# Attention and Mish FFN on one core: two weight pieces in turn on VectorE, gl moved from GpSimd to VectorE, chunk 2's normalising and moves spread over steps

## The chip, the cores and the metric

One Trainium2 chip, one of its cores. The kernel is one launch. The metric is the device time of that launch in microseconds, the median of several runs; times of single instructions come from one profiled execution, whose clock starts at the first instruction. TensorE multiplies matrices, VectorE, ScalarE and GpSimd work on whole tiles, SyncE only issues DMAs here. Each engine works its own instructions in the order of the program, and waits on semaphores for what others make.

## The reference

Windowed attention (each position sees itself and the 63 before it), then a feed-forward layer with Mish. Eight sequences of 576 positions, eight heads of 64.

```python
scores = (1 / sqrt(D)) * q @ k.T                    # per batch and head
mask   = (rel >= 0) & (rel < 64)                    # rel = pos[:, None] - pos[None, :]
attn   = softmax(where(mask, scores, -1e9))
x      = (attn @ v).transpose(0, 2, 1, 3).reshape(4608, 512)
h      = x @ w_in                                   # 512 x 2048
g      = h * tanh(softplus(h))                      # Mish
out    = g @ w_out                                  # 2048 x 512
```

## The kernel before

**Tiles.** The 4608 tokens are twelve chunks of 384. A chunk's attention runs over four pairs of heads: scores on TensorE into PSUM (`s_ps`), mask and row maximum on VectorE (`masked`: the instruction on `s_ps` and `mask`, shown as ISA in the order of instructions and as CUSTOM_DVE in the profile), exponentials on ScalarE (`exp`), normalising on VectorE (`normal`: two small instructions on `sm` and one on `pr`), a transpose, and the products with v (`o_ps`). The result is split into a high part `xh` and a low part `xl`.

**The feed-forward layer** is made in steps, one for each chunk c and each of 16 slices f of 128 hidden units. A step's input products are twelve matmuls (`h_ps`: xh with the high weights, xl with the high ones, xh with the low ones) into one of two PSUM banks with the tag "h_ps". `function` makes of them on ScalarE `t` (Mish) and `gh` (Mish, rounded to the matmul's type), and the residue `gl = t - gh` on GpSimd. Two steps later `flush` adds the step's nine output products to `acc` (gh with the high weights, gh with the low ones, gl with the high ones).

**Weights** come as 64-bit words in 32 pieces of 128x512 (`st`, three buffers) and are made into float pieces in stages, spread over the steps:

- `w_load` issues a piece's DMA on SyncE;
- `w_abs` takes the absolute bits of the high word (`wa`, a buffer of the tag "t" with four buffers, which `t` and `o` share);
- `w_bits` has four parts on VectorE, each working in place on `wa`: 0 and 1 are TENSOR_SCALAR, 2 and 3 SCALAR_TENSOR_TENSOR, of which part 3 is the last reader of `st`;
- `w_round` is ScalarE's copy into the high weights (`wi_h`, `wo_h`);
- `w_rest` is VectorE's subtraction that gives the low weights (`wi_l`, `wo_l`).

**The order.** In the head, units u = 0 to 7 are the attention of chunks 0 and 1, and pieces are worked in between. Then 32 steps of chunks 0 and 1 alternate (numbers n = 0 to 31 below; "step n" is one turn of the last loop). While `held[0]` is set, which it is for these 32, each engine's instructions keep the order in which the code issues them. A turn runs: the step's input products, t, gh and gl; `w_round`, `w_bits`, `w_abs`, `w_load`; a flush; `between(n)`; `w_rest`. In `between`, the attention of chunk 2 is made: at steps 8, 11, 17 and 20 (SCORES) the score products of one pair are put into both h banks and a second flush follows; VectorE reads them out (`masked`); at every second of these ScalarE makes both pairs' exponentials and VectorE normalises both. At 14, 17, 22 and 24 (MOVED) VectorE transposes one pair in blocks of 32 and SyncE moves the blocks with twelve DMAs (`pT<-tr`). The values of chunk 2 follow at steps 29 to 31 and after. From step 32 on a planner puts the attention of later chunks between the steps; the change leaves that code alone.

Of the kernel before, what the change touches and what calls it, by code (L numbers as in the profile page):

```python
# [10 lines left out]
F32 = mybir.dt.float32  # L11
# [4 lines left out]
ALU = mybir.AluOpType  # L16

P = 128
BLK = 64
# [8 lines left out]
def tile_window_attn_mish_ffn(  # L28
# [11 lines left out]
    NPAIR, _, NT = qT.shape  # L40
    NF, _, NC_, _ = w_in.shape
# [44 lines left out]
    pTs = [const.tile([P, P // 32, HM, 32], F32, name=f"pT{i}") for i in range(2)]  # L86
    for t in pTs:
        nc.gpsimd.memset(t, 0.0)
    pTs = itertools.cycle(pTs)
# [4 lines left out]
    held = [True]  # L94
# [17 lines left out]
    vec, act, pool, load = (InTurn(e) for e in (nc.vector, nc.scalar, nc.gpsimd, nc.sync))  # L112
# [10 lines left out]
    def acc_bank(t, name):  # L123
        return ps_acc.tile([P, CH], F32, name=name, tag=f"acc{t}")
# [107 lines left out]
        second = probs(c, s_ps[1], late)  # L232
        return [probs(c, s_ps[0], BY_HEAD), second]

    def moves(pT, tr):
        return [load.dma_start(pT[k:k + 32, r // 32, :, :], tr[r:r + 32, k // 32, :, :])
                for r in range(0, P, 32) for k in range(0, P, 32) if 0 <= k - r % BLK <= BLK]

    def run_transpose(pr, pT=None):
        tr = mp.tile([P, P // 32, HM, 32], F32, name="tr", tag="st", bufs=3) if pT is None else             ap_.tile([P, P // 32, HM, 32], F32, name="tr", tag="v_t", bufs=2)  # L240
        pT = pT or next(pTs)
        vec.transpose(tr.rearrange("p k j i -> p j k i"), pr.rearrange("p j (k i) -> p j k i", i=32))
        return pT, moves(pT, tr)

    def spare_pT():
        pT = mp.tile([P, P // 32, HM, 32], F32, name="pT", tag="st", bufs=3)
        pool.memset(pT, 0.0)
        return pT
# [28 lines left out]
    def att_transpose(pr):  # L277
        pT = next(pTs)
        tr = ap_.tile([P, P // 32, HM, 32], F32, name="tr", tag="pr", bufs=2)
        vec.transpose(tr.rearrange("p k j i -> p j k i"), pr.rearrange("p j (k i) -> p j k i", i=32))  # L280
        return pT, moves(pT, tr)

    def te_transpose(pr, banks):
        pT = next(pTs)
# [29 lines left out]
    def function(h_ps):  # L314
        t = mp.tile([P, CH], F32, name="t", tag="t", bufs=4)
        gh = mp.tile([P, CH], F32R, name="gh", bufs=3)
        gl = mp.tile([P, CH], F32R, name="gl", bufs=3)

        with tc.high_priority(offset=SOON):
            act.activation(t, h_ps, AF.Mish)  # L320
            act.activation(gh, h_ps, AF.Mish)
            pool.tensor_tensor(gl, t, gh.bitcast(F32), ALU.subtract)
        return gh, gl

    def ffn_out(acc, gg, f):
        gh, gl = gg
# [31 lines left out]
    loaded, worked, rounded = [], [], []  # L358

    def w_load():  # L360
        if pieces:
            fn, f = pieces.pop(0)
            loaded.append(fn(f))

    def w_abs(by_act):

        if not loaded:
            return
        st, wh, wl, first = loaded.pop(0)
        words = st.bitcast(U32).rearrange("p (n two) -> p n two", two=2)  # L370
        lo, hi = words[:, :, 0], words[:, :, 1]
        a = mp.tile([P, WP], U32, name="wa", tag="t", bufs=4)
        af = a.bitcast(F32)
        if by_act:
            act.activation(af, hi.bitcast(F32), AF.Abs)
        else:
            vec.tensor_scalar(a, hi, 0x7FFFFFFF, None, ALU.bitwise_and)
        worked.append((lo, hi, a, af, wh, wl))

    def w_bits(parts=range(4)):  # L380

        if not worked:
            return
        lo, hi, a, af, wh, wl = worked[0]
        for part in parts:
            if part == 0:
                vec.tensor_scalar(af, af, BIG, TINY, ALU.min, ALU.max)
            elif part == 1:
                vec.tensor_scalar(a, a, 3, 0x3FFFFFFF, ALU.logical_shift_left, ALU.bitwise_and)
            elif part == 2:  # L390
                vec.scalar_tensor_tensor(a, hi, 0xC0000000, a, ALU.bitwise_and, ALU.bitwise_or)
            else:
                vec.scalar_tensor_tensor(a, lo, 29, a, ALU.logical_shift_right, ALU.bitwise_or)
                rounded.append([af, wh, wl, False])
                worked.pop(0)

    def w_round():
        for r in rounded:
# [4 lines left out]
    def w_rest():  # L403
        while rounded and rounded[0][3]:
            af, wh, wl, _ = rounded.pop(0)
            vec.tensor_tensor(wl, af, wh.bitcast(F32), ALU.subtract)


    class Att:
        def __init__(self, c):  # L410
# [20 lines left out]
            self.load(p + 2, "qk")  # L431

        def transpose(self, p):
            self.pT[p] = att_transpose(self.pr.pop(p))

        def values(self, p, bank=at_bank, then_load=True):
            with in_order():
# [24 lines left out]
            self.pT[p] = te_copies(*self.pT[p], by)  # L462

        def dve_transpose(self, p, spare):
            self.pT[p] = run_transpose(self.pr.pop(p)[0], spare_pT() if spare else next(pTs))

        def run_scores(self, p):
            ps = (p, p + 1)
# [4 lines left out]

        def run_transpose(self, p):
            for q in (p, p + 1):
                self.pT[q] = run_transpose(self.pr.pop(q))

        def run_values(self, p):
            ps = (p, p + 1)
# [54 lines left out]
    U = len(units)  # L534
# [15 lines left out]
    def values_of(u):  # L550
        a, p = units[u]
        o_ps = (at_bank if u == U - 1 else lambda n: acc_bank(2, n))("o_ps")
        outs[u] = o_ps
        with in_order():
            value_products(a.v[p], a.pT.pop(p), [o_ps[:, n:n + BLK] for n in range(0, CH, BLK)])
        if u + 2 < U:
            a.load(p + 2, "v")
# [38 lines left out]
    for u in range(U + 1):  # L596
        now = u < U
        if u > 1:
            rest_high(u - 2)
        if now:  # L600
            a, p = units[u]
            squares_ = BY_PAIR if u == 0 else BY_HEAD
            a.masked(p, squares_, exps=False)
            exp(a.pr[p], squares_[:4])
        if u == 0:
            w_abs(False)
        if u > 1:
            rest_low(u - 2)
        if u + 1 < U:
            products_of(u + 1)  # L610
        if u > 0:
            units[u - 1][0].te_copies(units[u - 1][1], (act.copy, act.copy))
            values_of(u - 1)
        if u >= EARLY and len(early) < HEAD:
            early.append(first_half(len(early)))
        if now:
            exp(a.pr[p], squares_[4:])
        if u == U - 1:
            for n, h_ps in enumerate(early):
                step(n, h_ps)  # L620
        w_bits([0])
        w_rest()
        w_bits([1, 2])
        n = normal_parts(u) if now else iter(())
        next(n, None)
        w_bits([3])
        next(n, None)
        if u == U:
            rest_high(u - 1)
            rest_low(u - 1)  # L630
        if u + 1 not in WITHOUT:
            w_abs(u + 1 < U)
            w_load()
        next(n, None)
        w_round()
        if now:
            a.te_transpose(p, [at_bank("t_ps") if u == U - 1 else acc_bank(h, "t_ps") if u == U - 2 else h_bank("t_ps") for h in range(2)])
# [11 lines left out]
    third = atts[2]  # L649
    SCORES = [8, 11, 17, 20]  # L650
    MOVED = [14, 17, 22, 24]

    def between(n):

        if n in SCORES:
            p = SCORES.index(n)
            third.products(p, [h_bank("s_ps") for _ in range(2)])
            third.load(p + 2, "qk")
            with in_order():
                flush()  # L660
            third.masked(p, BY_HEAD, exps=False)
            if p % 2:
                third.exp(p - 1)
                third.exp(p)
                third.normal(p - 1)
                third.normal(p)
        if n in MOVED:
            p = MOVED.index(n)
            third.dve_transpose(p, p > 1)

    for n, (c, f) in enumerate(steps):
        held[0] = n < starts[2] // 2
        if n >= starts[2] // 2 and f == 0:

            while any(fn.__self__ is atts[c] for _, _, fn, _ in events):
                run(events[0][0])
        if n == starts[2] // 2:
            held[0] = True
            third.values(NPAIR - 1, h_bank)
            with in_order():  # L680
                flush()
            held[0] = False
        if n >= HEAD:
            step(n)
        run(2 * n)
        if held[0]:
            w_round()
            w_bits()
            w_abs(False)
            w_load()  # L690
            if last - 3 <= n < last - 1:
                third.load(n - last + 3, "v")
            if last < n < last + NPAIR:
                third.values(n - last - 1, h_bank)
        if len(pend) > LAG:
            with in_order():
                flush()
        if held[0]:
            between(n)
            w_rest()  # L700
        run(2 * n + 1)
    while pend:
        with in_order():
# [36 lines left out]
```

## Time and profile before

| | us |
|---|---|
| median of 3 runs | 942.03 |
| lowest to highest | 940.72 to 942.58 |
| the profiled execution's own time | 941.38 |
| its span, first to last instruction | 939.6 |
| TensorE matmul busy | 904.7 (96%) |
| VectorE busy | 315.8 (34%) |
| ScalarE busy | 397.1 (42%) |
| GpSimd busy | 204.1 (22%) |

Busy shares are over the whole span, and matmuls overlap, so TensorE's 96% doesn't say how near its peak it is. The profile's chain of waits goes through TensorE for 85% of the span, through VectorE for 8%, through DMA and SyncE for some 4%.

### The profile page before, as it was taken

What the parts mean: (1) busy time and instruction counts of PE and PEld (TensorE: products, weight loads), DVE (VectorE), ACT (ScalarE), POOL (GpSimd) and SP (SyncE); (2) the same over time, 40 slices, a digit from 0 to 9 for tenths busy, and PEclk for the clock granted to TensorE, in tenths of its full rate; (3) what the DMA queues carried; (4) which work ended last, traced back from release to release, by engine and by line L of the source; (5) the groups of instructions that cost most, each with busy time, mean ns of one, the idle gap of its engine ahead of it and who ended that gap; (6) DMA issues with size and microseconds to landing.
All of it is one profiled execution on the core that took longest, in us unless ns stands there. A gap on an engine that the chain in (4) does not pass through costs nothing.

```text
span 939.6 us, 16749 instructions
## 1 busy us (share of the span) xinstructions
PE 904.7 (96%) x6384; PEld 810.8 (86%) x6384; DVE 315.8 (34%) x1022; ACT 397.1 (42%) x1116; POOL 204.1 (22%) x211
## 2 busy tenths in 40 slices
PE   4698989999999999999999999999999999999998
PEld 3587979888889999889989999999998999999997
DVE  6989898313330330321321312303303213210000
ACT  5852626236642542542533524525525425432211
POOL 1021213222212122212222122221222122222221
PEclk9899989999999999999999999999999999999999
DMA  7744342232231321321222213203202312200000
GB/s 252 243 137 152 109 146 96 53 111 92 85 90 52 93 75 59 88 79 60 84 69 74 80 37 108 76 22 123 78 26 89 112 26 83 81 26 1 34 1 34
DMA packets 84943, 78.44 MB, mean 83 GB/s; under 512 B 11136, under 2 KB 76160, under 8 KB 84864
## 3 DMA queue, kind: packets, MB, share of 16 engines
q1 hardware_dynamic: 79680, 67.94, 23.7%
q10 hardware_dynamic: 5184, 9.44, 2.7%
q8 instruction: 51, 0.84, 0.4%
q14 instruction: 28, 0.23, 0.1%
HBM read 56.10 MB, written 9.44 MB: 70 GB/s over the span
## 4 chain that ended last, share of the span: by engine, by line
PE 85%; DVE 8%; DMA 2%; ACT 2%; SPq 2%; issue 1%; ACTq 0%
PE h_ps L115 40%; PE acc L115 38%; DVE wa L106 6%; PE o_ps L115 4%; PE s_ps L115 3%; SPq L106 2%; DMA st<-w_out 1%; ACT pr L106 1%; DVE pr L106 1%; DMA k_t<-kT 1%; DVE wo_l L106 0%; DVE wi_l L106 0%; ACT L106 0%; DVE xl L106 0%; DVE tr L106 0%
## 5 line engine op out<-in xcount | busy, mean ns | idle before, releaser
L106 POOL TENSOR_TENSOR gl<-t,gh 128x384 fp32r<-128x384 f32 x192 | 198.3, 1033 | 726.0 <-ACT gh L106 710.5
L106 ACT ACTIVATE t<-h_ps 128x384 f32<-128x384 f32 x192 | 94.4, 492 | 447.8 <-PE h_ps L115 433.1
L115 PE MATMUL h_ps<-xh,wi_h 128*128 128x384 f32 x768 | 261.5, 340 | 6.9 <-DVE mx L106 6.9
L115 PE MATMUL h_ps<-xh,wi_l 128*128 128x384 f32 x768 | 261.0, 340 | 0.0
L115 PE MATMUL h_ps<-xl,wi_h 128*128 128x384 f32 x768 | 259.7, 338 | 0.0
L115 PE MATMUL acc<-wo_h,gh 128*128 128x512 f32 x576 | 228.8, 397 | 0.0
L115 PE MATMUL acc<-wo_l,gh 128*128 128x512 f32 x576 | 226.8, 394 | 0.0
L115 PE MATMUL acc<-wo_h,gl 128*128 128x512 f32 x576 | 223.1, 389 | 0.0
L115 PEld LDWEIGHTS h_ps<-xh,wi_h 128*128 128x128 f32 x768 | 145.7, 190 | 16.3 <-issue 8.2
L115 PEld LDWEIGHTS h_ps<-xl,wi_h 128*128 128x128 f32 x768 | 145.7, 190 | 7.0
L115 PEld LDWEIGHTS h_ps<-xh,wi_l 128*128 128x128 f32 x768 | 145.4, 189 | 0.0
L115 PEld LDWEIGHTS acc<-wo_h,gl 128*128 128x128 f32 x576 | 108.1, 188 | 24.3 <-issue 0.2
L115 PEld LDWEIGHTS acc<-wo_h,gh 128*128 128x128 f32 x576 | 108.0, 187 | 20.9 <-issue 3.6
L115 PEld LDWEIGHTS acc<-wo_l,gh 128*128 128x128 f32 x576 | 108.3, 188 | 14.8
L270 DVE CAST xh<-o_ps 128x256 fp32r<-128x256 f32 x16 | 6.8, 425 | 326.5 <-PE o_ps L115 326.5
L106 ACT ACTIVATE pr<-pr,mx 128x128 f32<-128x128 f32 x288 | 111.7, 390 | 6.3 <-DVE mx L106 6.0
L106 ACT ACTIVATE gh<-h_ps 128x384 fp32r<-128x384 f32 x192 | 93.2, 485 | 0.0
L106 DVE CUSTOM_DVE_ANT_0 pr<-s_ps,mask 128x128 f32<-128x128 f32 x288 | 63.2, 286 | 24.6 <-PE s_ps L115 19.5
L340 DVE COPY o<-acc 128x512 f32<-128x512 f32 x12 | 8.3, 692 | 166.2 <-PE acc L115 166.2
L106 ACT ACT_TABLE_LOAD x45 | 57.7, 1283 | 6.0 <-DVE mx L106 5.1
L106 DVE SCALAR_TENSOR_TENSOR wa<-st,wa 128x512 uint32<-128x512 uint32 x64 | 54.1, 845 | 2.0
L106 ACT ACTIVATION_READ_ACCUMULATOR pr<-pr,mx 128x1 f32 x288 | 54.1, 188 | 0.0
(39 smaller groups left out, 465.3 us busy)
## 6 DMA issues: line engine op xcount, KB each, us to landing
v_t<-vN SPq DMA_DIRECT2D x48, 384.0 KB, 4.0
pT<-tr SPq DMA_DIRECT2D x480, 24.0 KB, 1.8
k_t<-kT SPq DMA_DIRECT2D x47, 224.0 KB, 4.3
out<-o ACTq DMA_DIRECT2D x36, 256.0 KB, 2.5
q_t<-qT SPq DMA_DIRECT2D x47, 192.0 KB, 4.1
st<-w_in SPq DMA_DIRECT2D x16, 512.0 KB, 3.5
st<-w_out SPq DMA_DIRECT2D x16, 512.0 KB, 3.5
q_t<-qT SPq DMA_DIRECT2D x3, 64.0 KB, 1.9
```

The costliest lines, as they stand in the source:

```text
L106: i = call(*args, **kw)
L115: order.append(nc.tensor.matmul(*args, **kw).ins)
L270: nc.vector.tensor_copy(xh[:, :cut], o_ps[0])
L340: nc.vector.tensor_copy(o, acc[t])
```

## The change

**What it does.** While the 32 steps run, `function` no longer issues gl on GpSimd but notes it in `residues`, and `residue()` issues it on VectorE. `w_bits` finds for each part the piece that has reached it (a counter at the end of its entry), and `weights()` calls the parts so that those of the new piece and of the one before it stand in turn. In a scores step `weights()` comes after `between(n)`, in the others before the flush, where `w_bits` and `w_abs` stood. Each of the two normalisings comes in a step of its own, one and two steps after the exponentials. The twelve moves of a transposed pair are a generator, from which each step takes four.

```diff
         with tc.high_priority(offset=SOON):
             act.activation(t, h_ps, AF.Mish)
             act.activation(gh, h_ps, AF.Mish)
-            pool.tensor_tensor(gl, t, gh.bitcast(F32), ALU.subtract)
+            if held[0]:
+                residues.append((gl, t, gh))
+            else:
+                pool.tensor_tensor(gl, t, gh.bitcast(F32), ALU.subtract)
+    def residue():
+        while residues:
+            gl, t, gh = residues.pop(0)
+            vec.tensor_tensor(gl, t, gh.bitcast(F32), ALU.subtract)
...
         for part in parts:
+            at = next((i for i, w in enumerate(worked) if w[-1] == part), None)
+            if at is None:
+                continue
+            lo, hi, a, af, wh, wl, _ = worked[at]
+            worked[at][-1] += 1
...
+        if u == U:
+            residue()
...
+    def weights():
+        residue()
+        w_abs(False)
+        w_bits([2])
+        w_rest()
+        w_bits([0, 3, 1])
+        w_load()
+
+    def some_moves():
+        if slow:
+            each, moved = slow.pop(0)
+            moved.extend(itertools.islice(each, 4))
...
             if p % 2:
                 third.exp(p - 1)
                 third.exp(p)
-                third.normal(p - 1)
-                third.normal(p)
+        if n - 1 in SCORES[1::2]:
+            third.normal(SCORES.index(n - 1) - 1)
+        if n - 2 in SCORES[1::2]:
+            third.normal(SCORES.index(n - 2))
...
+    w_bits([0, 1])
     for n, (c, f) in enumerate(steps):
...
             w_round()
-            w_bits()
-            w_abs(False)
-            w_load()
+            if n not in SCORES:
+                weights()
...
         if held[0]:
             between(n)
-            w_rest()
+            if n in SCORES:
+                weights()
+            some_moves()
         run(2 * n + 1)
```

**VectorE, steps 7 and 8, before.** The number behind `wa` tells the pieces apart; `s_ps_1061` are the scores of step 8. The four parts of one piece follow each other, and the scores are read behind the parts and the abs of step 8.

```order
L106 SCALAR_TENSOR_TENSOR wa_972<-st_895,wa_972 128x512 x2
L106 TENSOR_SCALAR wa_1010<-st_933 128x512
L106 TENSOR_TENSOR wo_l_105<-wa_931,wo_h_104 128x512
L106 TENSOR_SCALAR wa_1010<-wa_1010 128x512 x2
L106 SCALAR_TENSOR_TENSOR wa_1010<-st_933,wa_1010 128x512 x2
L106 TENSOR_SCALAR wa_1048<-st_974 128x512
L106 ISA pr_1088,mx_1089<-s_ps_1061,mask_82 128x128
L106 ISA mx_1089 128x1
```

**The same place of the change**, step 7 from its gl on, then the reads of step 8 (`s_ps_1054`) and the beginning of step 8's weights, with the equal reads between left out.

```order
L106 TENSOR_TENSOR gl_1003<-t_1001,gh_1002 128x384
L106 TENSOR_SCALAR wa_1008<-st_936 128x512
L106 SCALAR_TENSOR_TENSOR wa_970<-st_898,wa_970 128x512
L106 TENSOR_TENSOR wo_l_105<-wa_929,wo_h_104 128x512
L106 TENSOR_SCALAR wa_1008<-wa_1008 128x512
L106 SCALAR_TENSOR_TENSOR wa_970<-st_898,wa_970 128x512
L106 TENSOR_SCALAR wa_1008<-wa_1008 128x512
L106 ISA pr_1081,mx_1082<-s_ps_1054,mask_82 128x128
...
L106 TENSOR_TENSOR gl_1041<-t_1039,gh_1040 128x384
L106 TENSOR_SCALAR wa_1091<-st_977 128x512
```

The scores are now read ahead of all of step 8's weights, instructions of two pieces alternate, and each step begins with its gl.

**SyncE, the end of chunk 2's moves and the loads of v, before** (`v_t_1877` is pair 0 of chunk 2, `v_t_1907` pair 1, `v_t_2010` pair 2, `v_t_2055` pair 3).

```order
L106 DMA pT_1761<-tr_1763 32x192 x12
L106 DMA pT_1841<-tr_1843 32x192 x12
L106 DMA v_t_1877<-vN 128x6x128
L106 DMA v_t_1907<-vN 128x6x128
L106 DMA v_t_2010<-vN 128x6x128
```

**The same of the change** (pair 0 is `v_t_1865`, pair 1 `v_t_1899`).

```order
L106 DMA pT_1764<-tr_1766 32x192 x12
L106 DMA v_t_1865<-vN 128x6x128
L106 DMA pT_1838<-tr_1840 32x192 x4
L106 DMA v_t_1899<-vN 128x6x128
L106 DMA pT_1838<-tr_1840 32x192 x8
L106 DMA v_t_2010<-vN 128x6x128
```

Pair 0's load has moved ahead of the last pair's twelve moves, and pair 1's load stands between them. `v_t_1899` lies in the buffer of `v_t_1865`, since the other one still holds `tr_1840`; before, it had the other buffer.

## Rows read from the trace of the kernel before

**Rows 1.** Page, busy tenths in 40 slices of 23.5 us: VectorE.
```profile
DVE  6989898313330330321321312303303213210000
```

**Rows 2.** Busy time by stretch; the columns are named in the first line.
```profile
core 0: us, PE busy (x) PEld busy (x) DVE busy (x) ACT busy (x) POOL busy (x), PEclk, DMA share, GB/s
59.62:84.71 25.09, 25.09 (x127) 22.58 (x125) 24.44 (x41) 9.86 (x21) 6.68 (x7) 1.00 0.40 133
85.80:97.05 11.25, 8.14 (x35) 7.44 (x34) 9.45 (x28) 2.00 (x4) 0.96 (x1) 0.85 0.52 168
130.73:143.91 13.18, 9.39 (x36) 8.68 (x34) 10.57 (x29) 2.00 (x4) 1.01 (x1) 0.74 0.47 170
151.31:157.68 6.37, 6.37 (x35) 5.98 (x34) 4.34 (x19) 6.27 (x27) 0.00 (x0) 1.00 0.44 144
```

**Rows 3.** Timeline of TensorE: start, length, what, in brackets idle before and releaser.
```profile
84.71 1.15 PE L115 MATMUL s_ps<-k_t,q_t 64*64 64x128 f32 x24
...
87.75 0.39 PE L115 MATMUL acc<-wo_h,gl 128*128 128x512 f32 x1
91.25 0.41 PE L115 MATMUL h_ps<-xh,wi_h 128*128 128x384 f32 x1 [3.10 <-DVE mx L106]
...
130.73 0.50 PE L115 MATMUL acc<-wo_h,gh 128*128 128x512 f32 x1
...
136.87 0.66 PE L115 MATMUL h_ps<-xh,wi_h 128*128 128x384 f32 x1 [3.79 <-DVE mx L106]
...
187.99 0.92 PE L115 MATMUL o_ps<-pT,v_t 128*64 128x64 f32 x24 [0.98 <-ACT gh L106]
```

**Rows 4.** Timeline of VectorE ahead of the first stall.
```profile
84.85 2.10 DVE L106 SCALAR_TENSOR_TENSOR wa<-st,wa 128x512 uint32<-128x512 uint32 x2
86.86 0.42 DVE L106 TENSOR_SCALAR wa<-st 128x512 uint32<-128x512 uint32 x1
87.19 0.69 DVE L106 TENSOR_TENSOR wo_l<-wa,wo_h 128x512 fp32r<-128x512 f32 x1
87.80 0.88 DVE L106 TENSOR_SCALAR wa<-wa 128x512 f32<-128x512 f32 x2
88.72 1.42 DVE L106 SCALAR_TENSOR_TENSOR wa<-st,wa 128x512 uint32<-128x512 uint32 x2
90.05 0.42 DVE L106 TENSOR_SCALAR wa<-st 128x512 uint32<-128x512 uint32 x1
90.39 0.28 DVE L106 CUSTOM_DVE_ANT_0 pr<-s_ps,mask 128x128 f32<-128x128 f32 x1
```

**Rows 5.** Timeline of VectorE ahead of the second stall.
```profile
135.67 0.43 DVE L106 TENSOR_SCALAR wa<-st 128x512 uint32<-128x512 uint32 x1 [1.26 <-DMA st<-w_out]
```

**Rows 6.** Timeline of SyncE's DMA queue there.
```profile
123.77 8.02 SPq L106 DMA_DIRECT2D pT<-tr  x12
131.88 0.53 SPq L106 DMA_DIRECT2D st<-w_out  x1
```

**Rows 7.** Timeline of GpSimd at the same time as rows 4.
```profile
84.64 1.03 POOL L106 TENSOR_TENSOR gl<-t,gh 128x384 fp32r<-128x384 f32 x1 [2.83 <-issue]
```

**Rows 8.** Timeline of VectorE at other places: head's end, a normalising, a transpose.
```profile
56.50 0.55 DVE L106 TENSOR_TENSOR xl<-o_ps,xh 128x384 fp32r<-128x384 f32 x1
56.97 0.42 DVE L106 TENSOR_SCALAR wa<-st 128x512 uint32<-128x512 uint32 x1
...
106.62 0.17 DVE L106 TENSOR_SCALAR sm<-sm 128x6 f32<-128x6 f32 x1 [0.54 <-ACT pr L106]
...
107.05 0.96 DVE L106 TENSOR_TENSOR pr<-pr,sm 128x768 f32<-128x768 f32 x1
...
122.72 0.96 DVE L106 STREAM_TRANSPOSE tr<-pr 128x768 f32<-128x768 f32 x1
```

**Rows 9.** Timeline of ScalarE behind step 11's exponentials.
```profile
110.28 0.49 ACT L106 ACTIVATE t<-h_ps 128x384 f32<-128x384 f32 x1
```

**Rows 10.** Page, DMA issues: count, KB each, median us from issue to landing.
```profile
v_t<-vN SPq DMA_DIRECT2D x48, 384.0 KB, 4.0
...
st<-w_out SPq DMA_DIRECT2D x16, 512.0 KB, 3.5
```

More of the change, by code (lines that the diff above doesn't have):

```diff
@@ L233, in run_scores, with each_move @@
         return [probs(c, s_ps[0], BY_HEAD), second]
-    def moves(pT, tr):
-        return [load.dma_start(pT[k:k + 32, r // 32, :, :], tr[r:r + 32, k // 32, :, :])
-                for r in range(0, P, 32) for k in range(0, P, 32) if 0 <= k - r % BLK <= BLK]
+    def each_move(pT, tr):
+        for r in range(0, P, 32):
+            for k in range(0, P, 32):
+                if 0 <= k - r % BLK <= BLK:
+                    yield load.dma_start(pT[k:k + 32, r // 32, :, :], tr[r:r + 32, k // 32, :, :])
     def run_transpose(pr, pT=None):
@@ L242, in run_transpose @@
         vec.transpose(tr.rearrange("p k j i -> p j k i"), pr.rearrange("p j (k i) -> p j k i", i=32))
-        return pT, moves(pT, tr)
+        return pT, each_move(pT, tr)
     def spare_pT():
@@ L280, in att_transpose @@
         vec.transpose(tr.rearrange("p k j i -> p j k i"), pr.rearrange("p j (k i) -> p j k i", i=32))
-        return pT, moves(pT, tr)
+        return pT, each_move(pT, tr)
     def te_transpose(pr, banks):
@@ L321, in function @@
             act.activation(gh, h_ps, AF.Mish)
-            pool.tensor_tensor(gl, t, gh.bitcast(F32), ALU.subtract)
+            if held[0]:
+                residues.append((gl, t, gh))
+            else:
+                pool.tensor_tensor(gl, t, gh.bitcast(F32), ALU.subtract)
         return gh, gl
+    residues = []
+    def residue():
+        while residues:
+            gl, t, gh = residues.pop(0)
+            vec.tensor_tensor(gl, t, gh.bitcast(F32), ALU.subtract)
     def ffn_out(acc, gg, f):
@@ L377, in w_abs @@
             vec.tensor_scalar(a, hi, 0x7FFFFFFF, None, ALU.bitwise_and)
-        worked.append((lo, hi, a, af, wh, wl))
+        worked.append([lo, hi, a, af, wh, wl, 0])
     def w_bits(parts=range(4)):
-        if not worked:
-            return
-        lo, hi, a, af, wh, wl = worked[0]
         for part in parts:
+            at = next((i for i, w in enumerate(worked) if w[-1] == part), None)
[3 more added lines that the diff above has]
+            worked[at][-1] += 1
             if part == 0:
@@ L394, in w_bits @@
                 rounded.append([af, wh, wl, False])
-                worked.pop(0)
+                worked.pop(at)
     def w_round():
@@ L406, in w_rest @@
             vec.tensor_tensor(wl, af, wh.bitcast(F32), ALU.subtract)
+    slow = []
     class Att:
@@ L433, in transpose @@
         def transpose(self, p):
-            self.pT[p] = att_transpose(self.pr.pop(p))
+            pT, each = att_transpose(self.pr.pop(p))
+            self.pT[p] = pT, list(each)
         def values(self, p, bank=at_bank, then_load=True):
@@ L464, in dve_transpose @@
         def dve_transpose(self, p, spare):
-            self.pT[p] = run_transpose(self.pr.pop(p)[0], spare_pT() if spare else next(pTs))
+            pT, each = run_transpose(self.pr.pop(p)[0], spare_pT() if spare else next(pTs))
+            moved = []
+            self.pT[p] = pT, moved
+            slow.extend([(each, moved)] * 3)
         def run_scores(self, p):
@@ L475, in run_transpose @@
             for q in (p, p + 1):
-                self.pT[q] = run_transpose(self.pr.pop(q))
+                pT, each = run_transpose(self.pr.pop(q))
+                self.pT[q] = pT, list(each)
         def run_values(self, p):
```

## The prediction

> **What bounds the kernel now.** I read the busy slices first: VectorE is at nine tenths only in the first quarter of the span and nearly idle after it [rows 1]. So the place to look is the stage in which weights are made, 57 to 190 us. There TensorE's own pace is the floor: six steps of chunks 0 and 1 from 59.62 to 84.71 take 25.09 us, 4.17 us a step or 2.09 for each half, at full clock [rows 2]. Next I looked in TensorE's timeline for the places where that pace breaks. There are three [rows 3]: an input product starts 3.10 us late at 91.25, another 3.79 us late at 136.87, and the first value products of chunk 2 0.98 us late at 187.99.
>
> The first two have one cause. They come right after a scores step (8 and 17). The scores of chunk 2 lie in the two h banks, and the next input product may write a bank only when VectorE has read the scores out of it (the instructions on s_ps and mask, below "the reads"). The products of step 8 end at 85.86 (84.71 and 1.15 us), yet the first read starts at 90.39 [rows 3, 4], 4.5 us later, because VectorE is still busy with weights. At 135.67 it waits 1.26 us for a piece's load as well [rows 5], which SyncE issued at 131.88, behind twelve moves of a transposed tile that held its queue for 8.02 us [rows 6].
>
> Behind each of the two stalls the granted clock is not always the full 2.4 GHz: its mean over the stall and the two input products after it is 0.85 and 0.74, so part of them ran at 1.2 GHz. The stretch "nine output products, two input products" takes 11.25 and 13.18 us there and 6.37 at 151.31, where TensorE doesn't wait [rows 2]. The two places cost 4.88 and 6.81, together 11.7 us. The third costs its 1.0 us alone. That is all there is to win here: 12.7 us.
>
> **The change, part by part.** *VectorE's step.* Before, a piece takes on VectorE three TENSOR_SCALAR, two SCALAR_TENSOR_TENSOR and one TENSOR_TENSOR of 128x512, most of them waiting for the one just before. Two things lengthen this. An instruction whose follower waits for it is followed after its end: the two TENSOR_SCALAR of 87.80 take 0.92 to the next start, 0.46 each, while the one of 86.86 (0.42 long), whose follower does not need it, is followed after 0.33 [rows 4]. And a SCALAR_TENSOR_TENSOR pair that meets GpSimd's gl (84.64 to 85.67) takes 2.01 to the next start, the one at 88.72 without gl 1.33 [rows 4, 7]: 0.68 us for each piece.
>
> After the change VectorE's row is gl, abs, then parts of two pieces in turn, so that no instruction waits for its neighbour, and GpSimd has nothing to do. At the spacings without waits: three TENSOR_SCALAR at 0.33, two SCALAR_TENSOR_TENSOR at 0.60 (the pair's 1.42 is two of 0.69 and a wait of 0.04; without waits each is followed 0.09 before its end), one TENSOR_TENSOR at 0.61 (87.19 to 87.80), and gl. gl on VectorE isn't in the trace; the nearest row is xl, also 128x384, followed after 0.47 (56.50 to 56.97) [rows 4, 8]. Sum 0.99 + 1.20 + 0.61 + 0.47 = 3.27 us a step. Upper bound: each as if its follower waited, 3 x 0.46 + 2 x 0.73 + 0.73 + 0.60 = 4.17. I take 3.3, because the trace has both kinds of spacing for the same instruction.
>
> The Trainium skill, page "VectorE: DVE Perf Modes", section "The DRAIN you can't avoid", speaks against this: the next instruction starts only when the pipeline has emptied, and semaphores between chained instructions cost nothing extra (it sends the reader to another section for instructions that aren't held). By it the step would be the 4.17, by the rows 3.3. By the rows here it does not hold as it stands, since the follower at 87.19 starts 0.09 us before its forerunner's end.
>
> *The start.* Two gl before the last head pieces delay VectorE by 2 x 0.47: abs of the piece at 56.97 [rows 8] comes at 57.9, its two first parts run until 59.2, steps 0 and 1 have no gl (2.8 each), and gl of step 2 starts at 64.8 and ends at 65.4. Two things wait for it. The output products with gl of step 2 stand last in a block that is due at 65.89 (59.62 and three halves), so at 67.3. And t has one free buffer: ScalarE's next t waits for gl, ends gh 0.9 us later at 66.3, and the input product of step 5 is due at 67.96 in that bank. 1.6 us are left, and each step VectorE gains 0.9 us on TensorE. Cost nothing.
>
> *Scores steps.* The reads now stand ahead of the step's weights. VectorE ends step 7 at 64.8 + 6 x 3.3 = 84.6, before the products end (85.86). The first bank's three reads are over 0.7 us later, at 86.6, and its input product is due at 87.98 (87.75 and 0.23). The first stall goes. Step 17 is tighter, because gl now chains VectorE to ScalarE: in step 11 ScalarE loads a table, makes twelve exponentials and loads another, before t of step 12 at 110.28 [rows 9]; t and gh take 0.49 each, so gl of step 12 can start only at 111.2. Behind it in VectorE's queue stand five steps of weights (16.5), two normalisings (0.43 to the large instruction and 0.87 for it, 2.6 in all) and a transpose (0.87) [rows 8]: 131.2. The reads of step 17 then free the first bank at 131.9, due 132.9 (130.73 [rows 3] and 2.18 for a block of output products that nothing holds up). 1.0 us is left. The second stall goes too, with little to spare; VectorE's step may be 3.5 at most.
>
> *Moves and loads on SyncE.* Four moves a step take 4 x 0.67 = 2.7 us of the queue [rows 6], beside one load of a piece, within 4.17. So a load is no longer held up for 8 us. For the values, v of pair 0 stands behind twelve moves instead of 24, some 8 us earlier, and with 4.0 us to landing [rows 10] it is there before 187: the 0.98 us go. But v of pair 1 is now issued only when TensorE has read pair 0's v (same buffer): about 0.9 after the value products start, landing at 4.9, due at 0.9 + 2 x 2.09 = 5.1. Eight moves follow it (5.4), then v of pair 2: issued at about 6.7, landing at 10.7, due at 10.2. Cost between 0 and 1.0; I take 0.3, since v's median of 4.0 counts loads of busier stretches too.
>
> *Sum.* The profiled execution took 941.38 (span 939.6): 941.38 - 11.7 - 1.0 + 0.3 = 929.0. The median of the runs, 942.03, lies 0.65 above the profiled one, so 929.6 is forecast.
>
> **Rivals.** *A stall stays at a scores step.* Step 17 has 1.0 us of room, which five VectorE steps share; at 3.7 a step the room is gone, and one more wait for a load, 1.26 as now, makes a stall of that length, behind which the clock may fall as it did. It speaks for it that VectorE waited for a load just there [rows 5]. The price is between 1 and the 6.81 us of that place: 930.5 to 936.5.
>
> *Two pieces in turn gain nothing.* At 4.17 a step VectorE never makes up its lag: step 7 ends at 64.8 + 6 x 4.17 = 89.8, as late as now (90.39), step 17 likewise, and both stalls return with their clock. Only the third stall's 1 us and the 0.6 at the first are won: 940.4 on the median. Against it: the two spacings in rows 4.
>
> *Slower: the load of a piece paces VectorE.* A piece's buffer is free after its last part. Before, 7.7 us of VectorE's work lay between that and the abs that needs the new load (two contended steps); now it is one TENSOR_SCALAR, one step and a gl, 0.33 + 3.3 + 0.47 = 4.1 us. Loads take 3.5 [rows 10], the slow one of 131.88 3.8 [rows 5, 6]. If they took L, VectorE's step would be L - 0.8, and TensorE's pace is lost from L = 5.0 on. Over some 22 steps the whole gain is gone at L = 5.55; at 6.0, 22 x 1.03 = 22.7 us are lost against 12.4 gained: 952. Nothing in the rows shows loads that slow.
>
> **Numbers.** Forecast, both early stalls gone: 0.66, own range 928 to 931. A stall stays: 0.21, 930.5 to 936.5 and a little beyond. Gains nothing: 0.06, 940 to 942. Slower: 0.07, 944 to 955. A measurement of this kernel can tell about 0.2%, 1.9 us, from no change. Faster by more 0.88, within 0.05, slower 0.07. The range that leaves out 2 in 10 is 927.8 to 936: the forecast's and three quarters of the first rival.
>
> **What would show it.** Right: no idle of TensorE over 1 us between 57 and 190, full clock there, reads of step 8 starting within 0.3 us of the products' end; VectorE's SCALAR_TENSOR_TENSOR near 0.69 us each instead of a mean lengthened by gl, and a step of 3.3 us where it doesn't wait; GpSimd without gl until chunk 2; SyncE's moves in fours. Wrong: VectorE waiting long for a load ahead of abs, or for ScalarE's gh right before a scores step; TensorE waiting for gl inside an output block; pair 1's or pair 2's value products waiting for v. The forecast falls if VectorE's step without waits is above 3.5.

## The result and the profile after

The changed kernel takes 929.08 us (median of 4 runs, 928.32 to 929.3), the kernel before beside it 942.27: ratio 0.9862, 95% interval 0.9845 to 0.9879. Forecast were 929.6 and a range of 927.8 to 936. The profiled execution took 928.32, its span is 926.5.

The page first: the busy slices of VectorE, the chain's shares, and the group of GpSimd's gl.

```profile
DVE  6989898222233032131230321312303303210000
PE 93%; DVE 2%; SPq 1%; DMA 1%; ACT 1%; issue 0%; ACTq 0%
L106 POOL TENSOR_TENSOR gl<-t,gh 128x384 fp32r<-128x384 f32 x160 | 162.2, 1014 | 599.6 <-ACT gh L106 598.3
```

The chain now goes through TensorE for 93% and through VectorE for 2% (85% and 8% before). GpSimd makes 160 of the 192 gl; the 32 of the first steps have left it. Next TensorE's timeline at the places of [rows 3]: step 8, the ends of step 17's scores, and the values of chunk 2.

```profile
84.24 1.15 PE L115 MATMUL s_ps<-k_t,q_t 64*64 64x128 f32 x24
...
87.28 0.39 PE L115 MATMUL acc<-wo_h,gl 128*128 128x512 f32 x1
87.51 0.33 PE L115 MATMUL h_ps<-xh,wi_h 128*128 128x384 f32 x1
...
124.29 1.15 PE L115 MATMUL s_ps<-k_t,q_t 64*64 64x128 f32 x24
127.56 0.33 PE L115 MATMUL h_ps<-xh,wi_h 128*128 128x384 f32 x1
...
174.78 0.92 PE L115 MATMUL o_ps<-pT,v_t 128*64 128x64 f32 x24
...
185.59 0.92 PE L115 MATMUL o_ps<-pT,v_t 128*64 128x64 f32 x24 [0.28 <-issue]
```

No input product behind scores waits any more. From scores to the next input product it takes 3.27 us at both places. Before, it took 6.54 at the first (84.71 to 91.25). The values of the first two pairs start without a wait, those of the third wait 0.28 us. The stretches around both former stalls, by time, with the columns of [rows 2]:

```profile
83.00:96.00 13.00, 13.00 (x85) 11.58 (x84) 11.93 (x35) 3.65 (x8) 0.00 (x0) 1.00 0.45 140
123.00:140.00 17.00, 17.00 (x121) 14.59 (x121) 16.00 (x50) 7.44 (x14) 0.00 (x0) 1.00 0.63 189
```

TensorE is busy throughout at the full 2.4 GHz, where the means were 0.85 and 0.74. VectorE's timeline gives one whole step (gl to gl), the chain to ScalarE's exponentials at step 12, and the first reads of steps 8, 17 and 20:

```profile
64.28 0.56 DVE L106 TENSOR_TENSOR gl<-t,gh 128x384 fp32r<-128x384 f32 x1
64.75 0.42 DVE L106 TENSOR_SCALAR wa<-st 128x512 uint32<-128x512 uint32 x1
65.08 0.69 DVE L106 SCALAR_TENSOR_TENSOR wa<-st,wa 128x512 uint32<-128x512 uint32 x1
65.68 0.69 DVE L106 TENSOR_TENSOR wi_l<-wa,wi_h 128x512 fp32r<-128x512 f32 x1
...
67.56 0.55 DVE L106 TENSOR_TENSOR gl<-t,gh 128x384 fp32r<-128x384 f32 x1
...
85.16 0.29 DVE L106 CUSTOM_DVE_ANT_0 pr<-s_ps,mask 128x128 f32<-128x128 f32 x1 [0.16 <-PE s_ps L115]
...
105.95 0.56 DVE L106 TENSOR_TENSOR gl<-t,gh 128x384 fp32r<-128x384 f32 x1 [2.38 <-ACT gh L106]
...
125.83 0.28 DVE L106 CUSTOM_DVE_ANT_0 pr<-s_ps,mask 128x128 f32<-128x128 f32 x1
...
138.98 0.29 DVE L106 CUSTOM_DVE_ANT_0 pr<-s_ps,mask 128x128 f32<-128x128 f32 x1 [0.79 <-PE s_ps L115]
```

The step is 67.56 - 64.28 = 3.28 us. At step 8 VectorE waits for the scores; before, the scores waited for it. Step 17 is the tight one: three reads at 0.21 to the next start free the first bank at 126.5, and it is due at 127.56, so 1.1 us are left. One window row, from gl of step 12 to the reads of step 20, shows how full VectorE (third number) is there:

```profile
105.95:138.98 33.03, 33.03 (x203) 29.40 (x201) 31.89 (x76) 12.89 (x26) 0.00 (x0) 1.00 0.46 141
```

It works 31.89 of 33.03 us. TensorE is the bound there, and VectorE is the next by 1.1 us. Most experiments below turn on this row. Last, SyncE's queue where [rows 6] had twelve moves in a row:

```profile
119.47 2.48 SPq L106 DMA_DIRECT2D pT<-tr  x4
122.33 1.33 SPq L106 DMA_DIRECT2D st<-w_out  x1
123.70 2.41 SPq L106 DMA_DIRECT2D pT<-tr  x4
126.22 0.53 SPq L106 DMA_DIRECT2D st<-w_in  x1
```

**Where the time came from.** The stage from the first input product of the 32 steps to the first values of chunk 2 can be read in TensorE's timeline of every kernel (before: 44.81 to 187.99, after: 44.02 to 174.78). It fell by 12.42 us. The three waits of [rows 3] are 7.87 of it (3.10, 3.79 and 0.98); most of the rest is the clock, whose means of 0.85 over 11.25 us and 0.74 over 13.18 us [rows 2] took up to 5.1. Another 0.79 of the spans' 13.1 lies in the head, ahead of that stage, and the rest of the program is the same within 0.2.

### The profile page after: what moved, and what is told of

Read it like the earlier page. It is cut to its first block, busy times and chain, and to the rows that moved or that the text cites. A ratio compares the mean times of both kernels' runs of the same rounds, so it can differ in the third digit from the quotient of the medians.

```text
span 926.5 us, 16744 instructions
## 1 busy us (share of the span) xinstructions
PE 898.4 (97%) x6384; PEld 805.3 (87%) x6384; DVE 308.2 (33%) x1054; ACT 398.4 (43%) x1116; POOL 168.1 (18%) x179
## 4 chain that ended last, share of the span: by engine, by line
PE 93%; DVE 2%; SPq 1%; DMA 1%; ACT 1%; issue 0%; ACTq 0%
PE acc L115 43%; PE h_ps L115 43%; PE o_ps L115 4%; PE s_ps L115 4%; SPq L106 1%; DVE pr L106 1%; DVE wa L106 1%; DMA k_t<-kT 1%; ACT pr L106 1%; DMA st<-w_out 0%; ACT pT L106 0%; DMA pT<-tr 0%; DVE xl L106 0%; DVE sm L106 0%; ACT L106 0%
## 5 line engine op out<-in xcount | busy, mean ns | idle before, releaser
L106 POOL TENSOR_TENSOR gl<-t,gh 128x384 fp32r<-128x384 f32 x160 | 162.2, 1014 | 599.6 <-ACT gh L106 598.3
L115 PE MATMUL s_ps<-k_t,q_t 64*64 64x128 f32 x1152 | 43.8, 287 | 8.8 <-DMA k_t<-kT 8.5
```

Of the source, the lines that this page charges most:

```text
L106: i = call(*args, **kw)
L115: order.append(nc.tensor.matmul(*args, **kw).ins)
```

## The experiments

All kernels but the changed one were timed against the kernel before on their chip (medians 940.78 to 940.98); the changed one stood beside 942.27, so its median compares with theirs only to some 1.5 us. The intervals of `after_gl_pool`, `after_normals_together` and `gl_twice_from_21` touch that of the changed kernel, and their medians alone don't tell them from it. The last columns are from the profiled execution: the start of the first input product, the stage as above, and how much longer it is than after the change. The head differs between executions by more than some edits do, so small effects are read from the stage. That is one execution: for `after_reads_last` and `after_in_row` it took 933.19 and 930.88 us, some 2 us less than the other three runs of each (935.24 to 935.9 and 932.85 to 933.36), so their stages may be low values.

| kernel | median us | ratio [95%] | stage starts | stage us | longer |
|---|---|---|---|---|---|
| before | 942.27 | 1 | 44.81 | 143.18 | 12.42 |
| changed | 929.08 | 0.9862 [0.9845, 0.9879] | 44.02 | 130.76 | 0 |
| only_reads_first | 936.07 | 0.9954 [0.9938, 0.9969] | 44.91 | 136.54 | 5.78 |
| only_moves_spread | 938.36 | 0.9974 [0.9962, 0.9985] | 45.34 | 139.87 | 9.11 |
| only_faster_step | 939.54 | 0.9983 [0.9973, 0.9992] | 44.13 | 141.98 | 11.22 |
| after_reads_last | 935.3 | 0.994 [0.9924, 0.9956] | 45.79 | 134.19 | 3.43 |
| after_moves_at_once | 940.32 | 0.9996 [0.9985, 1.0006] | 44.48 | 140.32 | 9.56 |
| after_in_row | 932.89 | 0.9908 [0.9894, 0.9923] | 44.63 | 132.27 | 1.51 |
| after_gl_pool | 930.75 | 0.9894 [0.9877, 0.991] | 46.33 | 131.62 | 0.86 |
| after_normals_together | 930.72 | 0.9894 [0.9877, 0.9912] | 44.98 | 131.27 | 0.51 |
| gl_twice_from_21 | 930.81 | 0.9893 [0.9877, 0.9909] | 45.22 | 131.16 | 0.40 |
| after_gl_twice_half | 933.01 | 0.9916 [0.9899, 0.9932] | 45.03 | 134.55 | 3.79 |
| after_gl_twice | 940.99 | 1.0004 [0.9994, 1.0013] | 45.02 | 141.94 | 11.18 |
| gl_pool_longer | 939.75 | 0.9989 [0.998, 0.9998] | 47.47 | 140.39 | 9.63 |

**First: the place of the reads or the shorter step?** Theory P says that reading the scores ahead of the weights brings the gain, and the shorter VectorE step only gives it room. Theory S says that the shorter step brings it.

`only_reads_first` is the kernel before with the reads ahead of the weights in the scores steps:

```diff
+            if n not in SCORES:
+                piece()                 # w_bits(); w_abs(False); w_load()
...
             third.masked(p, BY_HEAD, exps=False)
+            piece()
```

> The kernel before with one edit: at steps 8, 11, 17 and 20 VectorE reads the scores ahead of the step's w_bits and w_abs (and the piece's load is issued there), all else as before: gl on GpSimd, the parts of a piece in a row, both normalisings and all twelve moves at once. Theory P (the place of the reads wins, the shorter VectorE step only gives room): the reads of step 8 start where the step's first part stood, 87.8 instead of 90.4, so the first bank is free at 88.5, due 88.0: 0.5 us of wait instead of 3.1, and no lower clock. VectorE's step stays at 3.9 with gl beside it, so at step 17 about 0.9 and at step 20 about 1.5 us of wait remain, and the 1.0 us before the values. 942.3 - 11.7 + 2.9 = 933.5, between 931.5 and 937. Theory S (the shorter step wins): VectorE is as late as before, both stalls and their clock stay, 939 to 943.

936.07, within P's range: 4.75 of the gain. TensorE's waits between 55 and 200 us:

```profile
PE h_ps L115 <- DVE mx L106: 2.3, 3, 0.9
PE o_ps L115 <- ACT gh L106: 1.4, 1, 1.4
PE h_ps L115 <- ACT gh L106: 0.8, 1, 0.8
```

The two long waits are gone, but VectorE is still late at step after step. `after_reads_last` is the changed kernel with `weights()` ahead of the reads in every step:

```diff
-            if n not in SCORES:
-                weights()
+            weights()
...
-            if n in SCORES:
-                weights()
```

> The changed kernel with one part undone: the weights of a scores step stand ahead of the reads of the scores, as in all other steps. P: one VectorE step of 3.28 us comes ahead of each read. By the times of the changed kernel: step 8, VectorE free at 85.0 + 3.28, first bank free at 89.0, due 87.5: 1.5 us of wait. Step 11: free at 100.7, first bank 101.4, due 101.3: 0. Step 17: 125.8 + 3.3 + 0.7 = 129.8, due 127.6: 2.3. Step 20: 138.2 + 3.3 + 0.7 = 142.2, due 141.3: 0.9. Together 4.7 us, 933.8; up to 938 if the clock falls behind one of the waits. S: the step is as short as in the changed kernel, so within 1.5 us of it, at most 930.5.

935.3, again within P's range. TensorE's waits there are these:

```profile
PE h_ps L115 <- DVE mx L106: 3.3, 2, 2.3
```

Both stalls come back, shorter than in [rows 3], and without the fall of the clock. `after_gl_pool` puts gl back on GpSimd.

```diff
-            if held[0]:
-                residues.append((gl, t, gh))
-            else:
-                pool.tensor_tensor(gl, t, gh.bitcast(F32), ALU.subtract)
+            pool.tensor_tensor(gl, t, gh.bitcast(F32), ALU.subtract)
```

> The changed kernel with one part undone: gl of the 32 steps is GpSimd's again. VectorE loses the 0.47 us of gl and gets back what GpSimd's gl holds it up, 0.68 for a SCALAR_TENSOR_TENSOR pair before: 2.81 + 0.7 = 3.5 us a step, at most 2.81 + 1.05 = 3.9 if the whole of gl is lost. VectorE is still chained to ScalarE behind the exponentials, since w_rest waits for the copy that stands behind gh. P: step 8 has its reads within 0.5 us of the products' end; step 17 has 1.0 us of room less 4 steps of 0.2: no wait, at 3.9 a step 1.4 us of wait. 929 to 930.5: that gl is VectorE's is worth nothing or 1 us. S: GpSimd's hold was what made VectorE late, so a stall comes back at step 8 or 17, with its clock 934 or more.

930.75, 0.25 above P's range and far below S's 934; the stage is 0.86 longer. `after_gl_twice` makes each gl of the 32 steps twice on VectorE (the same line two times).

> The changed kernel with each gl of VectorE made twice (the second repeats the first, the result is the same): VectorE's step is 0.60 longer, 3.28 + 0.60 = 3.88, the step of the kernel before, and nothing else changes. It measures the room that the prediction gave step 17. P: by the times of the changed kernel VectorE ends step 7 at 85.0 + 6 x 0.6 less the 0.86 that it waited for a load = 87.7, first bank free at 88.5, due 87.5: 1.0 us of wait at step 8; step 17: five steps of 0.6 are 3.0, room 1.0: 2.0 us; step 20: three more steps less its 0.8 of waiting and the 2.0 that TensorE lost: about 0.5. Together 3.5 us: 932.6, up to 936 with a lower clock behind step 17. S: a step as long as before brings back both stalls in full, 939 or more.

940.99: the whole gain is gone, as S has it, and P's 932.6 (936 at most) is 8 us too low. TensorE's waits, and the stretch 123 to 140 that is at full clock in the changed kernel:

```profile
PE s_ps L115 <- ACT gh L106: 4.3, 2, 3.0
PE acc L115 <- DVE gl L106: 1.4, 1, 1.4
PE h_ps L115 <- ACT gh L106: 0.4, 1, 0.4
```

```profile
123.00:140.00 17.00, 13.96 (x70) 11.17 (x69) 16.90 (x44) 4.38 (x9) 0.00 (x0) 0.80 0.43 136
```

P counted 1.0, 2.0 and 0.5 us at the reads of steps 8, 17 and 20. TensorE waits some 6 us at four places, none of them for the reads, most of all at the scores themselves, whose bank waits for ScalarE's gh. On top comes the clock: a mean of 0.80 over 17.0 us takes up to 3.4 us. What came out is neither P nor S: three kernels went P's way and the fourth S's. The reads' place alone brings 4.75 us, everything but the reads' place 5.5, of some 13.

**Second: by which way does a late VectorE hold TensorE up?** Theory R: by the reads, and by gl, since t has one buffer, so that t of the next step, its gh and with it the bank wait for gl. `gl_pool_longer` takes the second way out: gl is on GpSimd, and VectorE is made as slow as with gl twice in another way.

```diff
             if part == 0:
                 vec.tensor_scalar(af, af, BIG, TINY, ALU.min, ALU.max)
+                if held[0]:
+                    vec.tensor_scalar(af[:, :256], af[:, :256], BIG, TINY, ALU.min, ALU.max)
```

> The changed kernel with gl back on GpSimd and, on top, the first half of part 0 (the clip) of each piece made twice while the 32 steps run, which alters no value. VectorE's step is then 3.64 (as measured with gl on GpSimd) and about 0.25 more, 3.9 us, the same as the 3.88 with gl made twice on VectorE, which gave 940.99. What differs is that no t waits for VectorE. Theory R (late VectorE holds TensorE up by two ways, by the reads of the scores and by gl, since t has one buffer and t of the next step, its gh and with it the h bank wait for gl): only the reads are late here, by 5 x 0.25 = 1.3 us more than with gl on GpSimd alone (930.75), so 931.5 to 933.5. Rival U (the length of VectorE's step alone decides, whatever it holds): as gl twice, 938 to 942.

939.75, as U expected, so R is wrong about the way (the step came out at 3.96 us rather than 3.9). ScalarE's timeline ahead of the scores of step 17, and TensorE's second bank of scores:

```profile
133.73 0.62 ACT L106 CAST wi_h<-wa 128x512 fp32r<-128x512 f32 x1 [3.43 <-DVE wa L106]
134.26 0.48 ACT L106 ACTIVATE t<-h_ps 128x384 f32<-128x384 f32 x1
134.64 0.48 ACT L106 ACTIVATE gh<-h_ps 128x384 fp32r<-128x384 f32 x1
```

```profile
135.18 0.87 PE L115 MATMUL s_ps<-k_t,q_t 64*64 64x128 f32 x12 [1.99 <-ACT gh L106]
```

TensorE waits 5.2 us in all: 1.43 and 1.99 for gh at the second bank of the scores of steps 8 and 17, 0.44 and 1.35 later. Behind the first of these the clock falls, which takes up to 3.4 us more (1.00 less 0.83, over 20):

```profile
80.00:100.00 20.00, 18.57 (x95) 16.07 (x94) 18.13 (x45) 6.19 (x14) 4.59 (x4) 0.83 0.47 154
```

There is a third way. `w_round`, ScalarE's copy of a worked piece, waits for VectorE, and t and gh of the next step stand behind it in ScalarE's queue. They start the moment the copy is done, and the bank waits for gh. The kernel before has the same order. No kernel was run in which ScalarE's copies did not wait for VectorE, so that this way carries all of the loss here is read from the trace, not shown by an edit.

`after_gl_twice_half` makes every second gl twice (a mean step of 3.58).

> The changed kernel with every second gl of the 32 steps made twice on VectorE: a mean step of 3.28 + 0.30 = 3.58 us. Theory R, with 1.0 us of room at step 17 that five steps share: 5 x 0.30 = 1.5 us later, 0.5 beyond the room there, nothing lost before: 929.3 to 931. Rival U': the loss is in proportion to the lengthening (0.60 a step cost 11.9 us, so 0.30 costs half of that): 934 to 936.

933.01: between R and U', nearer U'. TensorE waits once, 2.0 us at the scores of step 17, where R allowed 0.5 beyond the room; the rest of the 3.79 is mainly in matmuls that run slower behind it (mean granted clock 0.91 from 120 to 140). `gl_twice_from_21` makes gl twice only behind the last reads.

> The changed kernel with gl made twice on VectorE only from step 21 on, behind the last reads of scores (gl made twice in all 32 steps gave 940.99, 0.37 for each). Theory T (lateness costs where a bank is waited for, at the scores steps 8 and 17 above all): 929.1 to 930.7, the upper end for the one wait for gl of 1.40 us that the trace with all gl twice shows at 171. Rival U (each lengthening of a step costs, wherever it is): 11 x 0.37 = 4.1, so 933.

The stage is 0.40 longer, with one wait of 0.6 us for gl. U would have 4.1. So VectorE's time is dear up to step 20 and nearly free behind it.

**Third: the other parts of the change.** `after_in_row` works a piece's four parts in a row:

```diff
         residue()
+        w_bits()
         w_abs(False)
-        w_bits([2])
         w_rest()
-        w_bits([0, 3, 1])
         w_load()
...
-    w_bits([0, 1])
     for n, (c, f) in enumerate(steps):
```

> The changed kernel, but VectorE's row in a step is gl, parts 0 to 3 of one piece in a row, abs of the next, the subtraction: the two pieces aren't worked in turn. gl stays on VectorE and the reads stay ahead. By the two spacings of rows 4 the step is 0.47 + 0.46 + 0.46 + 0.73 + 0.60 + 0.33 + 0.61 = 3.66 us instead of 3.28. Theory R: 5 x 0.38 = 1.9 us later at step 17, 0.9 beyond the room: 930 to 932. Rival (an instruction that waits for its neighbour is followed no later than one that doesn't, so order within the step is worth nothing): 929.1 within 0.7, and a step of 3.3. Rival (the order of the two pieces carries the gain): 935 or more.

932.89, with the step as expected. VectorE's timeline, one step from gl to gl:

```profile
64.41 0.55 DVE L106 TENSOR_TENSOR gl<-t,gh 128x384 fp32r<-128x384 f32 x1
64.88 0.88 DVE L106 TENSOR_SCALAR wa<-wa 128x512 f32<-128x512 f32 x2
65.80 1.42 DVE L106 SCALAR_TENSOR_TENSOR wa<-st,wa 128x512 uint32<-128x512 uint32 x2
...
68.07 0.55 DVE L106 TENSOR_TENSOR gl<-t,gh 128x384 fp32r<-128x384 f32 x1
```

68.07 - 64.41 = 3.66 us, as worked out from [rows 4], against 3.28 in turn: the order of the same seven instructions is worth 0.38 us a step. The stage is 1.51 longer (R: 0.9) in that execution, the median 3.8 higher, so what the order costs the whole kernel is known only to lie between the two. `after_moves_at_once` issues the twelve moves of a pair in a row again, which is `moved.extend(each)` in the place of the line with `slow.extend`.

> The changed kernel with the twelve moves of a transposed pair issued at once, as before, instead of four a step. Theory T, by now: in the stage up to the values TensorE loses what VectorE's lateness beyond its room (1.0 us at step 17) makes it wait, and the clock behind a wait of 2 us or more may take up to 4 us on top. Here a piece's load stands behind 12 moves (8 us) in steps 14 and 17, so VectorE waits for it at the abs of steps 17 and 19 by some 2 and 4 us more; step 20 has 0.8 us of waiting and 1 us of room to take from, and v of pair 0 stands behind 24 moves as before, 1 us: 931 to 933, to 935 if the clock falls. Rival M (the moves matter for v alone): 930.1. Rival N (spreading the moves is worth nothing, TensorE has slack for it): 929.1.

940.32: this edit alone takes all of the gain, and no theory had it. SyncE's queue, VectorE's two waits, and TensorE:

```profile
119.89 8.31 SPq L106 DMA_DIRECT2D pT<-tr  x12
128.31 0.53 SPq L106 DMA_DIRECT2D st<-w_out  x1
...
130.43 7.62 SPq L106 DMA_DIRECT2D pT<-tr  x12
...
165.14 15.74 SPq L106 DMA_DIRECT2D pT<-tr  x24
```

```profile
132.35 0.43 DVE L106 TENSOR_SCALAR wa<-st 128x512 uint32<-128x512 uint32 x1 [3.42 <-DMA st<-w_out]
142.16 0.43 DVE L106 TENSOR_SCALAR wa<-st 128x512 uint32<-128x512 uint32 x1 [3.15 <-DMA st<-w_out]
```

```profile
145.84 0.41 PE L115 MATMUL h_ps<-xh,wi_h 128*128 128x384 f32 x1 [2.67 <-DVE mx L106]
...
184.80 1.31 PE L115 MATMUL o_ps<-pT,v_t 128*64 128x64 f32 x24 [3.66 <-issue]
```

VectorE's waits are as expected (6.57 us against some 6). They cost more than expected: 2.67 at the reads of step 20 (with 0.67 ahead and 1.34 behind, where TensorE waits for gh), and, because the last transposes are late too, v of pair 0 stands behind 24 moves that begin only at 165.14. The values wait 3.66 us instead of 1.0, and behind that wait, past the stage, the clock falls, which takes up to 1.7 us more (1.00 less 0.67, over 5.2):

```profile
184.80:190.00 5.20, 5.20 (x37) 4.43 (x38) 0.56 (x1) 0.48 (x1) 0.00 (x0) 0.67 0.36 107
```

`after_normals_together` puts both normalisings back right behind the exponentials.

```diff
                 third.exp(p)
-        if n - 1 in SCORES[1::2]:
-            third.normal(SCORES.index(n - 1) - 1)
-        if n - 2 in SCORES[1::2]:
-            third.normal(SCORES.index(n - 2))
+                third.normal(p - 1)
+                third.normal(p)
```

> The changed kernel with both normalisings of two pairs right behind their exponentials, as before, so that the weights of steps 11 and 20 stand behind VectorE's wait for ScalarE's exponentials. Theory T: the 2.3 us of weights of step 11 that now fill that wait come behind it, step 17's reads are 1 to 2.3 us later than the 1.0 us of room can take or just within it: 929.5 to 931.5, to 933.5 if the clock falls. Rival N (VectorE's order there is worth nothing, since its work in sum is the same): 929.1.

The stage is 0.51 longer, less than T. The median lies 1.6 above the changed kernel's, but this stage begins 0.96 later, and the intervals touch; a cost beyond the 0.5 is not shown.

**Fourth: parts done alone.** `only_faster_step` has gl on VectorE and two pieces in turn, and nothing else of the change (the edits of `after_reads_last`, `after_moves_at_once` and `after_normals_together` together). `only_moves_spread` is the kernel before with four moves a step:

```diff
-            self.pT[p] = run_transpose(self.pr.pop(p)[0], spare_pT() if spare else next(pTs))
+            pT, each = run_transpose(self.pr.pop(p)[0], spare_pT() if spare else next(pTs))
+            moved = []
+            self.pT[p] = pT, moved
+            slow.extend([(each, moved)] * 3)
...
             w_rest()
+            some_moves()
```

> The changed kernel with reads behind the weights, both normalisings right behind the exponentials and the twelve moves at once, as before: only gl on VectorE and the two pieces in turn are left of the change. Theory R: the two stalls of the reads behind the weights (935.3 measured with that alone undone), the late v of pair 0 (1.0), the normalisings (1 to 2) and waits for loads behind twelve moves (0 to 2) come on top: 937 to 940. Rival S (VectorE's faster step carries most of the gain by itself): 935.5 or less.

> The kernel before with the one change that the twelve moves of a transposed pair are issued four a step; gl stays on GpSimd, the reads stay behind the weights, pieces are worked in a row, both normalisings stay together. Theory T (edits count only together: a VectorE that is paced at 4.2 a step is late anyway, so that the load behind twelve moves costs it 1.26 us at most): 1.0 us for v of pair 0 and 0 to 1.3 of the second stall, 938.7 to 940. Rival W (the queue of moves is what makes step 17 and the values late, as it took all of the gain when put back into the changed kernel): the second stall's 6.8 and the 1.0 go, 933 to 935.

939.54, within R's range, and 938.36, near T's and far from W's. With the faster step alone VectorE stands still for a load, and TensorE for VectorE:

```profile
DVE wa L106 <- DMA st<-w_out: 6.3, 2, 4.9
```

```profile
PE h_ps L115 <- DVE mx L106: 6.6, 2, 4.7
```

A faster VectorE reaches the load behind the twelve moves earlier and waits longer for it: 4.9 us against 1.26 in [rows 5]. With the moves spread alone both stalls stay, the second shorter (3.1 and 2.5, before 3.10 and 3.79):

```profile
PE h_ps L115 <- DVE mx L106: 5.6, 2, 3.1
```

The three parts done alone gain 4.75, 2.4 and 1.4 us, 8.6 in sum, where all together, with the normalisings, gain 13.2. Undone alone, the moves cost 11.2, the reads 6.2, the order of the two pieces 3.8, gl's place 1.7 on the medians (to some 1.5 us, as said above), and 9.6, 3.4, 1.5 and 0.9 in the stage. The parts are not terms of a sum. By the traces each removes one way in which VectorE falls behind by more than the 1.1 us it has; the moves also hold up v.

## Why the prediction was right, and what in it was too small

- **VectorE's step**, 3.3 forecast, 3.28 measured, and 3.66 with the pieces in a row. The Trainium skill, page "VectorE: DVE Perf Modes", section "The DRAIN you can't avoid", lets the next instruction start only when the pipeline is empty, with or without a semaphore. Taken without the exception that it names, for instructions that aren't held, it gives both orders one length; the trace does not, by 0.38 us a step. So the rival that two pieces in turn gain nothing is out.
- **gl's place.** The prediction took 0.68 us a piece off for GpSimd's gl. With gl back on GpSimd, VectorE's instructions that meet it grow in this way (its timeline):

```profile
112.92 1.24 DVE L106 TENSOR_SCALAR wa<-st 128x512 uint32<-128x512 uint32 x1
...
117.85 0.42 DVE L106 TENSOR_SCALAR wa<-st 128x512 uint32<-128x512 uint32 x1
118.19 1.50 DVE L106 SCALAR_TENSOR_TENSOR wa<-st,wa 128x512 uint32<-128x512 uint32 x1
```

  The last is 0.8 more than 0.69; GpSimd's gl there starts at 117.85 and takes 1.29. The Trainium skill, page "SBUF — State Buffer", section "Who interferes with whom", says that a VectorE instruction with two SBUF inputs contends with a GpSimd one that reads SBUF; the row of 118.19 agrees. It is not the usual case here: of the 20 weight instructions that gl lengthens in this trace between 60 and 160 us, 15 are TENSOR_SCALAR with one input (0.42 to 1.24, as at 112.92), which that sentence doesn't cover. The step is 3.64 us there, 0.36 longer than with gl on VectorE.
- **The two stalls** are gone with their clock, the step that carried 11.7 us of the sum. Reads of step 8 start with the end of the scores. Step 17 has 1.1 us of room where 1.0 was forecast: gl of step 12 does wait for ScalarE, and the bank is free at 126.5 and due at 127.56 instead of 131.9 and 132.9, since the working had left the first stall in on both sides.
- **The values.** Pairs 0 and 1 find their v there, pair 2 waits 0.28, forecast 0.3. Four moves take 2.4 to 2.5 us of SyncE, forecast 2.7.
- **The sum**: 12.42 us measured in the stage, 12.7 forecast. The other 0.79 of the profiled executions' difference comes from the head, for which the change is not needed: heads in the same order begin the stage between 44.02 and 45.79, and the changed kernel's 44.02 is the earliest of the fourteen in the table. With the head of the kernel before, its profiled execution would have taken 929.1, where the sum gave 929.0. The agreement of the whole time to 0.5 us is better than heads that differ by 1.8 us allow one to count on.
- **Too small: the price of the moves.** The part on SyncE counted the moves for v's 1.0 us and, within the second stall, for a wait of 1.26. Undone they cost 11.2: 9.56 in the stage, 3.66 of it ahead of the values, and the clock behind it. The sum stayed right because all parts were made together.
- **Too small: the rival that a stall stays.** It put the room's end at 3.5 to 3.7 us a step and the price at 1 to 6.81. At 3.58 the stage is 3.79 longer, at 3.66 (in a row) 1.51, at 3.88 11.18. The bound was right, the price at 3.9 was not: several waits and the clock join. Nor does the mean step set the price alone, since 3.58 (every second gl twice) costs the stage more than 3.66.
- **The rival that loads pace VectorE** came nearer than the rows let expect: in the changed kernel a piece's load takes 3.3 us in the median and 4.9 at most, where that rival begins at 5.0. VectorE waits 1.1 us in all for loads, and TensorE doesn't wait for it.

## What to carry to other kernels

Before a stall is put down to the place of one read, count the busy time of the engine that is late over the whole stretch between two of its forced waits: here it was full to 1.1 us in 33, so that no part of the change could be priced by itself. Follow a late engine through the other engines' queues as well; a copy that another engine makes of its results can hold up what stands behind that copy. And long runs of small DMAs on the queue that also issues loads are best cut into pieces, the more so the faster the engine is that waits for the loads.

## What the runs showed of the hardware that was not expected

The head, whose order of instructions `after_reads_last` shares with the changed kernel, does not take the same time in two executions. The stretch 20 to 55 us, first in the changed kernel, then in `after_reads_last`:

```profile
20.00:55.00 35.00, 22.45 (x333) 18.36 (x325) 30.74 (x113) 29.14 (x100) 0.00 (x0) 0.95 0.68 221
```

```profile
20.00:55.00 35.00, 26.26 (x330) 21.77 (x328) 30.77 (x113) 30.11 (x106) 0.00 (x0) 0.80 0.70 226
```

TensorE is busy 22.45 and 26.26 us there, at a mean granted clock of 0.95 and 0.80, and the stage behind it begins 1.8 us later. Why the clock differs between the two stays open. Nor does the length of a wait of TensorE tell here whether the clock falls behind it: it fell behind 1.43 us in `gl_pool_longer`, and not behind 2.29 in `after_reads_last` or 2.67 in `after_moves_at_once`. A comparison of whole times that is after less than 2 us should first look at the head.
